# The scale of w_in from sums of magnitudes by ScalarE's accumulator, in place of maxima by VectorE

## The chip, the cores and the metric

The kernel runs on one core of a Trainium2 chip. The time is the device time in microseconds of one execution, the median of three runs. The core has five engines that matter here: TensorE (PE) multiplies matrices, VectorE (DVE) and ScalarE (ACT) work on elements, GpSimd (POOL) does sums and reductions over partitions, and SyncE (SP) issues the transfers by DMA. Each engine works through its own instructions in their order; semaphores make one engine wait for another.

## The reference

Attention with random features comes first, over 8 batches, 8 heads, 576 rows and 64 columns; then a two-layer network over its output, as 4608 rows of 512.

```python
scale = 1.0 / np.sqrt(np.sqrt(D))
q_s, k_s = (q * scale, k * scale)

def phi(x):
    proj = np.einsum('bhsd,md->bhsm', x, omega)      # omega is 128 x 64
    sq = np.sum(x * x, axis=-1, keepdims=True) / 2.0
    h = proj - sq
    h = h - np.max(h, axis=-1, keepdims=True)
    return np.exp(h) / np.sqrt(m)

q_p, k_p = (phi(q_s), phi(k_s))
kv = np.einsum('bhsm,bhsd->bhmd', k_p, v)
z = np.sum(k_p, axis=2)
num = np.einsum('bhsm,bhmd->bhsd', q_p, kv)
den = np.einsum('bhsm,bhm->bhs', q_p, z)[..., None] + 1e-06
x = (num / den).transpose(0, 2, 1, 3).reshape(4608, 512)

h = x @ w_in                                          # 512 x 2048
sp = np.where(h > 20.0, h, np.log1p(np.exp(np.minimum(h, 20.0))))
out = (h * np.tanh(sp)) @ w_out                       # 2048 x 512
```

Everything is float32, in and out.

## The kernel before, in words

**Numbers.** Most matmuls run on float16. Each float32 operand is split into two float16 parts, a high one and what is left, and three products of parts are summed. So that the parts stay in the range of float16, each operand is multiplied by a power of two first. For the activations that factor comes from constants (`HC` is one) and from the scales of the operands; for the weights it comes from the data: from the largest magnitude in `w_in`, and in `w_out`.

**Weights.** Each of the two weight matrices comes as eight blocks of 128 x 1024. A block is loaded as 64-bit words, and `w_task` (from L200) makes float32 out of them: ACT shifts the upper word by a Prelu (L211), DVE the lower one (L213), DVE joins them (L217, its result goes to a tile `w` or `wo`), and DVE reduces the block to the largest magnitude of each partition, one column of `wmax` (L221). When all eight blocks of a matrix are there, `w_scale` (L229) reduces `wmax` once more (`am`) and takes the largest over the partitions: for `w_in` by POOL (`pow2`, L156, which calls L118), for `w_out` by a PE transpose and a matmul that spreads the value again (`pow2_pe`: row_w L136, one_w L139, every_w L148). Then `w_split` (L244) makes the two float16 parts of each block, the high one on ACT (L74), the rest on DVE (L85).

**Rows and chunks.** The 4608 rows go in 18 chunks of 256. For each chunk, `ff_in` (L763, matmuls into `ph`) multiplies by `w_in`, the nonlinearity follows on ACT and DVE (result `g`), and `ff_out` (matmuls into `po`) multiplies by `w_out`. The last three chunks use a scheme with seven products in place of eight (`ff_in7`, `ff_out7`). Chunk 0, and the first feature tiles, are computed in float32 directly, since the split weights don't exist yet: `ff_in` for it reads the unsplit `w` (L782), `ff_out0` (L1113, matmuls at L1129) the unsplit `wo`.

**Features.** `features` (L385) makes a tile of q or k features: PE multiplies by omega (`pq`, `pk`: L426 in float32, L411 in float16), DVE takes the maximum of each row (`mxq`, `mxk`, L436), ACT the exponentials (`eq`, `ek`, L441 and L451). k features are multiplied with v into `pkv` (L500), whose evicted form is `kvf` or `kv`. q features are transposed, by PE in the first tiles (`pt`, L677, evicted as `qp`) and by DMA later (`qp<-qn`), and multiplied with kv (`pn`, L688 and L584); DVE divides (L692 to L698) and gives the rows `x`, whose transpose (`px`, then `xT`) goes into `ff_in`. At the start PE also runs matmuls without a use (`spin`, L101), some of which wait for the same data as real ones.

**Order.** The program is written as generators, each of which yields when it has issued a step; an agenda of slots decides which goes on next, by start tables and by the number that each yields (a later slot). A scheduler with priorities then orders each engine's instructions, and `behind(...)` (L194) ties an instruction behind the n-th matmul of a list of anchors; the tables `AN`, `AO`, `AP` and `AM` hold such numbers for the steps of `w_task`.

Of the kernel before, what the change touches and what calls it, by code (L numbers as in the profile page):

```python
# [9 lines left out]
F16 = mybir.dt.float16  # L10
# [4 lines left out]
AF = mybir.ActivationFunctionType  # L15
ALU = mybir.AluOpType
AX = mybir.AxisListType
# [5 lines left out]
TOP = 2.0 ** 14  # L23
KVC = 2.0 ** -23
TX = 2.0 ** 12
HC = 2.0 ** -22
LNT = math.log(TOP)


# [1 line left out]
def tile_kernel(  # L31
    ctx: ExitStack,
    tc: tile.TileContext,
    qT: bass.AP,
    kT: bass.AP,
    vL: bass.AP,
    omT: bass.AP,
    w_in: bass.AP,
    w_out: bass.AP,
    out: bass.AP,  # L40
):
    nc = tc.nc
    P = 128
# [18 lines left out]
    sb = ctx.enter_context(tc.tile_pool(name="sb", bufs=2))  # L62
# [6 lines left out]
    act, dve, pool = nc.scalar, nc.vector, nc.gpsimd  # L69
# [104 lines left out]
    BW = KT * DF // NB  # L174
# [3 lines left out]
    def flat32(slot):  # L178
        return slot.rearrange("p a b -> p (a b)").bitcast(F32)

    def fetch_w(n, i, dma):
        src = w_src[n](i)


        at = ({0: 0, 1: 1, 2: 2, 3: 3}, {7: 0, 6: 1, 3: 0})[n].get(i)
        if at is not None:
            raw = wo_t[:, 2 * at:2 * at + 2].rearrange("p a b c -> p (a b c)").bitcast(I64)
        else:
            raw = sb.tile([P, BW], I64, tag="g", name=f"raw{i}", bufs=GB)
        dma.dma_start(out=raw.rearrange("p (a b) -> p a b", b=src.shape[2]), in_=src)  # L190
        return raw

    @contextmanager
    def behind(nth, first=0):  # L194
        with ExitStack() as st:
            for ins in anchors.get(nth, ())[first:]:
                st.enter_context(tc.issue_after(ins))
            yield

    def w_task(i, name):  # L200

        n = 0 if name == "wi" else 1
        raw = loaded.pop(f"w{n}_{i}", None) or fetch_w(n, i, w_dma)
        yield W_LOAD
        word = raw.bitcast(I32).rearrange("p (n two) -> p n two", two=2)
        low, high = word[:, :, 0], word[:, :, 1]
        dst = flat32(slots[w_at(n, i)])
        di = dst.bitcast(I32)
        with behind(AP[i] if n == 0 else None):
            m = high.bitcast(F32)  # L210
            act.activation(m, m, AF.Prelu, scale=2.0 ** -112, alpha=-(2.0 ** 32))  # L211
        with behind((AN, AO)[n][i]):
            dve.tensor_single_scalar(out=di, in_=low, scalar=29, op=ALU.logical_shift_right)  # L213
        yield W_GAP
        did("w", n, i)
        with behind((AN, AO)[n][i]):
            dve.scalar_tensor_tensor(  # L217
                out=di, in0=high, scalar=3, in1=di, op0=ALU.logical_shift_left, op1=ALU.bitwise_or
            )
        with behind(AM[i] if n == 0 else None):  # L220
            dve.tensor_reduce(  # L221
                out=wmax[n][:, i:i + 1], in_=dst, axis=AX.X, op=ALU.max, apply_absolute_value=True
            )

    def w_at(n, i):

        return i + 1 if n == 0 else NB + i
# [37 lines left out]
    def did(*key):  # L265
        done[key] = done.get(key, 0) + 1
# [467 lines left out]
    def b_scales(b):  # L734


        if b not in scales:
# [6 lines left out]
            dve.scalar_tensor_tensor(  # L744
                out=us[:, 1:2], in0=s_v, scalar=HC * TX / TOP, in1=s_w[0], op0=ALU.mult, op1=ALU.mult
            )
# [6 lines left out]
    def o_scale(b):  # L753
        us = b_scales(b)
        if b not in done_o:
            done_o.add(b)
            dve.tensor_tensor(out=us[:, 2:3], in0=us[:, 0:1], in1=p_w[1], op=ALU.mult)
            dve.tensor_scalar_mul(us[:, 2:3], us[:, 2:3], 1.0 / (TX * HC))
        return us
# [397 lines left out]
    AO = (None,) * 8  # L1157
    AV = 3
    AN = (None,) * 5 + (31,) * 3
    AM = (None,) * 3 + (31,) * 5  # L1160
    AP = (None,) * 7 + (101,)

    W_LO = ('dddddddd', 'dddddddd')
    W_HI = ('aaaaaaaa', 'aaaaaaaa')
# [26 lines left out]
    wmax = []  # L1191
# [63 lines left out]
    for what in PREL.split():  # L1255
        i = int(what[1:] or 0)
# [12 lines left out]
    for i in range(NB):  # L1269
        start(w_task(i, "wi"), WIS[i])  # L1270
    for i in reversed(range(1, NB)):
        start(w_task(i, "wo"), WOS[i])
# [9 lines left out]
    next(fi, None)  # L1282
    fi, fo = ff_in(1), ff_out0()
    start(w_task(0, "wo"))
    at(slot[0] + W_LOAD + W_GAP + 2, scale_w, 1)
    for j in range(8):
# [75 lines left out]
```

## Time and profile before

| | |
|---|---|
| time, median of 3 runs | 940.65 us (939.26 to 940.75) |
| profiled execution, whole time | 941.74 us |
| its span, first to last instruction | 940.0 us |
| PE busy | 922.9 us, 98 % |
| DVE, ACT, POOL busy | 705.5, 658.9, 214.0 us |
| mean granted TensorE clock | 0.991 of full speed |

The durations below are from the one profiled execution. Its whole time is longer than its span by what lies before the first and behind the last instruction. In a row of a timeline, the time in brackets is how long the engine stood idle before the group, and what it waited for. Instructions on an engine overlap a little, so the distance between the starts of two equal instructions (the pitch) is shorter than the duration of one.

### The profile page before, as it was taken

To read this page: it belongs to the slowest core of one execution; us is meant where nothing else is said; L and a number is where in the kernel's file an instruction comes from. 1 tells how busy PE (TensorE), PEld (TensorE's weight loads), DVE (VectorE), ACT (ScalarE), POOL (GpSimd) and SP (SyncE) were. 2 spreads that over 40 slices of the span, in tenths; PEclk is the share of its full clock that TensorE was granted. 3 is DMA by queue.
4 is the path that set the end of the run, shared out by engine and by line. 5 is a ranking of instruction groups with operands and counts; after the bars stand their busy time and mean duration, and the time that the engine had idled before them with its cause. 6 is when DMAs were issued, how large, how long until landed. Compare 5 with 4: busy or idle time off the path is not lost. (4 is left out here: it accounts for less than half of the span.)

```text
span 940.0 us, 21111 instructions
## 1 busy us (share of the span) xinstructions
PE 922.9 (98%) x8795; PEld 690.8 (73%) x8795; DVE 705.5 (75%) x1234; ACT 658.9 (70%) x873; POOL 214.0 (23%) x134
## 2 busy tenths in 40 slices
PE   9699989999999999999999999999999999999998
PEld 6588865777777777777777777777777776679997
DVE  4799898686678688887688856878688666658774
ACT  5668976678786878778677786778787766345442
POOL 0000023252242123321233133231242232200000
PEclk9799999999999999999999999999999999999999
DMA  9867323532452255423543255422533146973521
GB/s 297 273 217 223 101 66 86 105 77 68 105 109 75 77 97 145 89 74 93 104 111 95 80 104 122 109 77 75 121 81 91 34 107 148 226 201 91 158 69 45
DMA packets 153055, 108.69 MB, mean 116 GB/s; under 512 B 112832, under 2 KB 125248, under 8 KB 152960
## 3 DMA queue, kind: packets, MB, share of 16 engines
q1 hardware_dynamic: 152640, 106.75, 44.3%
q8 instruction: 69, 1.13, 0.5%
q10 hardware_dynamic: 320, 0.59, 0.2%
q14 instruction: 26, 0.21, 0.1%
HBM read 63.14 MB, written 17.83 MB: 86 GB/s over the span
## 5 line engine op out<-in xcount | busy, mean ns | idle before, releaser
L782 PE MATMUL ph<-xT,w 128*128 128x256 f16 (+1 forms) x2816 | 342.2, 278 | 0.0
L1111 PE MATMUL po<-wo,g 128*128 128x512 f16 x1344 | 308.5, 379 | 0.0
L782 PEld LDWEIGHTS <-w 128*128 128x128 f16 x2688 | 260.7, 98 | 46.1 <-issue 0.6
L1111 PEld LDWEIGHTS <-g 128*128 128x128 f16 x1344 | 127.3, 98 | 132.7
L83 POOL TENSOR_TENSOR sq<-fq,sq 64x1024 f16<-64x1024 f32 x31 | 70.7, 2280 | 252.8 <-ACT sq L74 175.3
L969 ACT ACTIVATE h<-ph,us 128x512 f32<-128x512 f32 (+3 forms) x152 | 83.4, 573 | 50.6 <-PE ph L782 49.7
L85 DVE SCALAR_TENSOR_TENSOR g<-h,us,g 128x1024 f16<-128x1024 f32 (+3 forms) x76 | 98.7, 1309 | 15.2 <-ACT g L74 14.9
L83 POOL TENSOR_TENSOR sk<-fk,sk 64x1152 f16<-64x1152 f32 x24 | 59.4, 2474 | 91.8 <-ACT sk L74 84.2
L83 POOL TENSOR_TENSOR xs<-x,xs 128x512 f16<-128x512 f32 (+1 forms) x35 | 40.8, 1165 | 153.0 <-DVE xs L76 102.2
L969 ACT ACT_TABLE_LOAD x56 | 71.8, 1283 | 1.0
L451 ACT ACT_TABLE_LOAD x53 | 68.0, 1283 | 4.2 <-DVE ek L445 3.3
L436 DVE TENSOR_REDUCE mxq<-pq 128x4 f32<-128x512 f32 x72 | 46.7, 682 | 24.3 <-PE pq L411 23.3
L83 DVE TENSOR_TENSOR qn<-eq,qn 128x1024 f16<-128x1024 f32 x31 | 39.2, 1264 | 29.7 <-ACT qn L74 29.6
L919 PEld LDWEIGHTS <-w 128*128 128x128 f16 x1008 | 59.0, 98 | 3.0 <-issue 0.4
L74 ACT ACTIVATE g<-h,us 128x1024 f16<-128x1024 f32 (+3 forms) x64 | 58.1, 932 | 0.9
L451 ACT ACTIVATE ek<-ek,lnt 128x1152 f32<-128x1152 f32 x24 | 30.1, 1256 | 40.2 <-DVE ek L445 40.1
L436 DVE TENSOR_REDUCE mxk<-pk 128x4 f32<-128x512 f32 (+1 forms) x96 | 49.6, 548 | 9.8 <-PE pk L426 4.0
L83 DVE TENSOR_TENSOR kp<-ek,kp 128x1152 f16<-128x1152 f32 x24 | 32.8, 1366 | 25.7 <-ACT kp L74 25.7
L1058 PEld LDWEIGHTS <-gb 128*128 128x128 f16 x504 | 48.3, 98 | 5.2
L83 POOL TENSOR_TENSOR vb<-vf,vb 128x640 f16<-128x640 f32 x24 | 37.3, 1556 | 56.5 <-DVE vb L76 42.4
L451 ACT ACTIVATE eq<-eq,lnt 128x1024 f32<-128x1024 f32 x31 | 35.6, 1149 | 18.9 <-DVE eq L445 18.7
L969 ACT ACTIVATE h<-h,us 128x1024 f32<-128x1024 f32 (+2 forms) x16 | 14.7, 932 | 48.3 <-DVE h L929 48.3
(185 smaller groups left out, 1373.9 us busy)
## 6 DMA issues: line engine op xcount, KB each, us to landing
w<-ds SPq DMA_DIRECT2D x48, 256.0 KB, 3.5
vf<-in_vL_dram SPq DMA_DIRECT2D x32, 325.0 KB, 3.4
out_dram<-o SPq DMA_DIRECT2D x36, 256.0 KB, 2.4
fq<-in_qT_dram SPq DMA_DIRECT2D x31, 256.0 KB, 3.5
fk<-in_kT_dram SPq DMA_DIRECT2D x24, 256.0 KB, 3.7
raw<-in_w_out_dram SPq DMA_DIRECT2D x5, 1024.0 KB, 8.1
wo<-in_w_in_dram SPq DMA_DIRECT2D x4, 1024.0 KB, 10.9
raw<-in_w_in_dram SPq DMA_DIRECT2D x4, 1024.0 KB, 15.0
```

Source lines behind the costliest of these rows:

```text
L74: act.activation(out, in_, AF.Copy, scale=scale)
L83: eng.tensor_tensor(out=out, in0=in_, in1=hi, op=ALU.subtract)
L85: eng.scalar_tensor_tensor(out=out, in0=in_, scalar=scale, in1=hi, op0=ALU.mult, op1=ALU.subtract)
L436: sub = dve.tensor_reduce(out=mx[:, lo:hi], in_=pp[:, :m, :], axis=AX.X, op=ALU.max, negate=by_act)
L451: last = act.activation(e, e, AF.Exp, bias=lnt)
L782: last = nc.tensor.matmul(out=ph[:, i, :], lhsT=wi(a, k, f) if c else wi0(k, f), rhs=xT[c][:, y, k, :] if c else xT0()[:, k, :], start=n = ...
L919: last = nc.tensor.matmul(out=ph[:, i, :], lhsT=left(gr, op_l, i, a, k), rhs=x_region(c, r)[:, y, k0 + k, :], start=n == 0, stop=n == len( ...
L969: act.activation(h[:, :, lo:hi], ph[:, :, lo:hi], AF.Mish, scale=us[:, 0:1])
L1058: nc.tensor.matmul(out=ps, lhsT=gT[c, n][:, i, a, f, :], rhs=rhs, start=f == 0 and (a, y) == (1, 0), stop=f == FG - 1 and (a, y) == (0, 0),)
L1111: last = nc.tensor.matmul(out=po[i], lhsT=gT[c, gr][:, a, f % FG, i * P:(i + 1) * P], rhs=wo(y, f), start=f == 0 and (a, y) == parts[0], s ...
```

## The change

For `w_in` (n == 0) the column of `wmax` is no longer DVE's largest magnitude of a block's partition but the sum of the 1024 magnitudes: ACT takes Abs of the block into a scratch tile `rough`, which nothing reads, and its accumulator gives the sum. The largest over blocks and partitions is taken as before and rounded to a power of two. `w_out` keeps its maxima. As the sums are larger than the maxima, the parts of `w_in` become smaller, and the constant `HC` in the factors of the activations goes from 2^-22 to 2^-20. The scratch tile has the tag of `xs`, of which there are two buffers.

```diff
-HC = 2.0 ** -22
+HC = 2.0 ** -20
...
-        with behind(AM[i] if n == 0 else None):
-            dve.tensor_reduce(
-                out=wmax[n][:, i:i + 1], in_=dst, axis=AX.X, op=ALU.max, apply_absolute_value=True
-            )
+        if n == 0:
+            yield WSUM[i]
+            rough = sb.tile([P, BW], F16, tag="xs", name=f"rough{i}", bufs=2)
+            with behind(AP[i]):
+                act.activation(rough, dst, AF.Abs, accum_out=wmax[n][:, i:i + 1])
+            return
+        dve.tensor_reduce(
+            out=wmax[n][:, i:i + 1], in_=dst, axis=AX.X, op=ALU.max, apply_absolute_value=True
+        )
...
-    AM = (None,) * 3 + (31,) * 5
     AP = (None,) * 7 + (101,)
+    WSUM = (0,) * 8
```

The instructions of all engines stand in another order in about the first 175 us, and in the same order behind that. Lines behind the change have numbers that are five higher than before.

On DVE, ahead of the maxima of q's first tile (mxq) and before that tile's exponentials, the rows were these (w_104 is a block of `w_in`, vam and p_v belong to the scale of v):

```order
L217 SCALAR_TENSOR_TENSOR w_104<-wo,w_104 128x1024
L327 TENSOR_REDUCE vam_358<-vmx_353 128x1
L213 TENSOR_SCALAR w_105<-wo 128x1024
L161 TENSOR_SCALAR p_v_362<-allm_v_360 128x1
L221 TENSOR_REDUCE wmax_121<-w_104 128x1
L125 TENSOR_SCALAR p_v_362<-p_v_362 128x1
L436 TENSOR_REDUCE mxq_330<-pq_0_331 128x4
```

And now:

```order
L217 SCALAR_TENSOR_TENSOR w_104<-wo,w_104 128x1024
L332 TENSOR_REDUCE vam_359<-vmx_354 128x1
L213 TENSOR_SCALAR w_105<-wo 128x1024
L161 TENSOR_SCALAR p_v_363<-allm_v_361 128x1
L441 TENSOR_REDUCE mxq_331<-pq_0_332 128x4
L125 TENSOR_SCALAR p_v_363<-p_v_363 128x1
```

The maximum of block w_104 is gone from the place ahead of mxq, and so is that of the block before it, further up.

On ACT, between the transposed rows of chunk 0 (xT) and the exponentials of q's tile 2 (eq) with what follows them, the rows were these:

```order
L716 ACTIVATE xT_297<-px_481 128x4x128
L716 ACTIVATE xT_297<-px_487 128x4x128
L211 ACTIVATE raw_159<-raw_159 128x1024
L74 ACTIVATE g_0_634<-ph_0_0_0_635 128x512
L441 ACTIVATE eq_520<-pq_0_522,mxq_521 128x128 x4
L441 ACTIVATE eq_520<-pq_4_523,mxq_521 128x128 x4
L74 ACTIVATE qp_564<-pt_0_565 128x512
L74 ACTIVATE g_0_634<-ph_0_0_2_657 128x512
L441 ACTIVATE eq_532<-pq_0_534,mxq_533 128x128 x4
```

And now:

```order
L721 ACTIVATE xT_297<-px_491 128x4x128
L211 ACTIVATE raw_155<-raw_155 128x1024
L211 ACTIVATE raw_157<-raw_157 128x1024
L211 ACTIVATE raw_159<-raw_159 128x1024
L224 ACTIVATE rough_516,wmax_121<-w_108 128x1024
L224 ACTIVATE rough_521,wmax_121<-w_109 128x1024
L224 ACTIVATE rough_526,wmax_121<-w_110 128x1024
L446 ACTIVATE eq_528<-pq_0_530,mxq_529 128x128 x4
L446 ACTIVATE eq_528<-pq_4_531,mxq_529 128x128 x4
L446 ACTIVATE eq_540<-pq_0_542,mxq_541 128x128 x4
L446 ACTIVATE eq_540<-pq_4_543,mxq_541 128x128 x4
L74 ACTIVATE qp_572<-pt_0_573 128x512
```

Two Prelu (raw_155 and raw_157) that stood ahead of xT, and three Abs, now stand between xT and the exponentials, and all sixteen exponentials stand ahead of the first evicted qp; the g casts come later.

On PE, at the same place, from the last product with omega (pq) to the transposes (pt):

```order
L426 MATMUL pq_4_535<-om_f,fq_507 128x128
L782 MATMUL ph_0_0_0_635<-xT_297,w_103 128x256 x7
L782 MATMUL ph_0_0_2_657<-xT_297,w_104 128x256 x6
L677 MATMUL pt_0_565<-ident,eq_520 128x128 x4
L782 MATMUL ph_0_0_2_657<-xT_297,w_104 128x256 x2
L782 MATMUL ph_0_1_0_682<-xT_297,w_105 128x256
L677 MATMUL pt_1_571<-ident,eq_520 128x128 x4
```

And now:

```order
L431 MATMUL pq_4_543<-om_f,fq_512 128x128
L787 MATMUL ph_0_0_0_643<-xT_297,w_103 128x256 x4
L682 MATMUL pt_0_573<-ident,eq_528 128x128 x4
L787 MATMUL ph_0_0_2_665<-xT_297,w_104 128x256
L682 MATMUL pt_1_579<-ident,eq_528 128x128 x4
L787 MATMUL ph_0_0_2_665<-xT_297,w_104 128x256 x2
L682 MATMUL pt_0_586<-ident,eq_540 128x128 x4
```

Fewer matmuls of chunk 0 stand ahead of the first transposes (a matmul in float32 is two instructions in the profile); the others follow behind pn.

On PE, around every_w, the rows were these:

```order
L136 MATMUL row_w_1116<-ident,am_w_1114 1x128
L677 MATMUL pt_1_1108<-ident,eq_1042 128x128
L1129 MATMUL po_0_1387<-wo,g_1_785 128x512
L677 MATMUL pt_1_1108<-ident,eq_1042 128x128 x2
L1129 MATMUL po_0_1387<-wo,g_1_785 128x512
L148 MATMUL every_w_1122<-one_w_1118,idle 128x1
L688 MATMUL pn_0_1133<-kvf_162,qp_1101 64x65
```

And now:

```order
L787 MATMUL ph_0_1_2_1171<-xT_508,w_105 128x256
L787 LDWEIGHTS w_105
L787 MATMUL ph_0_1_2_1171<-xT_508,w_105 128x256
L148 MATMUL every_w_1130<-one_w_1126,idle 128x1
L693 MATMUL pn_0_1141<-kvf_162,qp_1109 64x65
```

No po of chunk 0 stands around every_w any more; matmuls of the next chunk's `ff_in` do.

## Rows read from the trace of the kernel before

**Rows 1.** The page: busy time of PE with its share of the span and its instructions, beside those of the other engines; then PE and the granted clock in 40 equal slices of the span, in tenths.

```profile
PE 922.9 (98%) x8795; PEld 690.8 (73%) x8795; DVE 705.5 (75%) x1234; ACT 658.9 (70%) x873; POOL 214.0 (23%) x134
...
PE   9699989999999999999999999999999999999998
...
PEclk9799999999999999999999999999999999999999
```

**Rows 2.** The waits of PE over the whole span: who waited for whom; us in total, times, longest us.

```profile
PE spin L101 <- ACT eq L441: 7.3, 1, 7.3
PE pn L584 <- DMA qp<-qn: 2.5, 3, 1.9
...
PE every_w L148 <- DVE one_w L139: 0.8, 1, 0.8
```

**Rows 3.** Windows: stretch, its length, busy time (and instructions) of PE, PEld, DVE, ACT and POOL, then the granted clock, the share of the DMA engines and GB/s.

```profile
25.00:26.00 1.00, 0.00 (x0) 0.00 (x0) 1.00 (x3) 0.34 (x1) 0.00 (x0) 1.00 1.05 385
26.00:27.00 1.00, 0.00 (x0) 0.00 (x0) 1.00 (x2) 0.61 (x1) 0.00 (x0) 0.81 1.03 381
27.00:28.00 1.00, 0.00 (x0) 0.00 (x0) 0.87 (x3) 0.55 (x1) 0.50 (x1) 0.50 1.05 387
...
39.00:40.00 1.00, 1.00 (x7) 0.69 (x5) 0.00 (x0) 0.93 (x3) 0.00 (x0) 0.50 1.05 269
40.00:41.00 1.00, 1.00 (x8) 0.81 (x7) 0.00 (x0) 1.00 (x4) 0.00 (x0) 0.86 1.02 296
```

**Rows 4.** The timeline of PE from 0 to 62 us: start, duration of the group, what it is, and the idle time before it.

```profile
14.36 2.44 PE L500 MATMUL pkv<-vf,ek 128*128 128x65 f32 x20
...
21.54 2.06 PE L426 MATMUL pq<-om_f,fq 64*128 64x128 f32 x32
30.87 1.22 PE L101 MATMUL spin<-eq,ident 128*128 128x256 f32 x2 [7.27 <-ACT eq L441]
31.88 4.36 PE L500 MATMUL pkv<-vf,ek 128*128 128x65 f32 x20
...
49.48 5.88 PE L782 MATMUL ph<-xT,w 128*128 128x256 f32 x26
55.83 0.66 PE L677 MATMUL pt<-ident,eq 128*128 128x128 f32 x4 [0.48 <-ACT eq L441]
```

**Rows 5.** The timeline of DVE, from 20 to 30 us.

```profile
20.76 1.21 DVE L221 TENSOR_REDUCE wmax<-w 128x1 f32<-128x1024 f32 x1
...
25.99 1.21 DVE L217 SCALAR_TENSOR_TENSOR w<-wo,w 128x1024 int32<-128x1024 int32 x1
...
28.22 1.21 DVE L221 TENSOR_REDUCE wmax<-w 128x1 f32<-128x1024 f32 x1
29.35 0.14 DVE L125 TENSOR_SCALAR p_v<-p_v 128x1 f32<-128x1 f32 x1
29.41 0.68 DVE L436 TENSOR_REDUCE mxq<-pq 128x4 f32<-128x512 f32 x1
```

**Rows 6.** The timeline of ACT, from 26 to 72 us.

```profile
26.39 1.16 ACT L211 ACTIVATE wo<-wo 128x1024 f32<-128x1024 f32 x1 [1.05 <-DMA wo<-in_w_in_dram]
30.19 2.18 ACT L441 ACTIVATE eq<-pq,mxq 128x128 f32<-128x128 f32 x8 [2.64 <-DVE s_v L127]
...
41.36 0.27 ACT L74 ACTIVATE kvf<-pkv 128x130 f32<-128x130 f32 x1
41.52 2.15 ACT L211 ACTIVATE raw<-raw 128x1024 f32<-128x1024 f32 x2
...
46.13 0.60 ACT L716 ACTIVATE xT<-px 128x512 f32<-128x512 f32 x1 [0.70 <-PE px L715]
...
54.64 1.14 ACT L441 ACTIVATE eq<-pq,mxq 128x128 f32<-128x128 f32 x4 [1.23 <-DVE mxq L436]
...
61.77 1.28 ACT L74 ACTIVATE w<-w,s_w 128x1024 f16<-128x1024 f32 x1
...
64.86 0.74 ACT L74 ACTIVATE xs<-x 128x512 f16<-128x512 f32 x1
...
71.24 0.60 ACT L74 ACTIVATE g<-ph 128x512 f32<-128x512 f32 x1 [0.87 <-PE ph L782]
```

**Rows 7.** Groups of instructions by line and form, from 0 to 110 us: count, then busy us and mean ns of one, then idle time before them.

```profile
L221 DVE TENSOR_REDUCE wmax<-w 128x1 f32<-128x1024 f32 x8 | 9.5, 1208 | 0.0
L211 ACT ACTIVATE raw<-raw 128x1024 f32<-128x1024 f32 x9 | 10.4, 1165 | 0.1
```

**Rows 8.** The timeline of PE from 117 to 161 us, and behind the dots the window from 144 to 146 us (columns as in rows 3).

```profile
119.98 0.38 PE L148 MATMUL every_w<-one_w,idle 1*128 1x1 f32 x2 [0.81 <-DVE one_w L139]
...
133.97 5.32 PE L1129 MATMUL po<-wo,g 128*128 128x512 f32 x12
141.17 0.92 PE L584 MATMUL pn<-kv,qp 128*128 128x65 f16 x24 [1.89 <-DMA qp<-qn]
...
143.95 14.19 PE L1129 MATMUL po<-wo,g 128*128 128x512 f32 x30
...
159.29 0.92 PE L584 MATMUL pn<-kv,qp 128*128 128x65 f16 x24 [0.29 <-DMA qp<-qn]
...
144.00:146.00 2.00, 2.00 (x4) 0.97 (x4) 1.95 (x6) 1.17 (x2) 1.27 (x1) 0.50 0.00 0
```

**Rows 9.** Transfers issued from 55 to 85 us: how many, and the median us from issue to landing.

```profile
xT<-xs SPq DMA_TRANSPOSE x2, 4.2
```

## The prediction, made blind

> **What bounds the kernel now.** I read the busy shares first. TensorE (PE) is busy 98 % of the span and every other engine 76 % or less [rows 1]; with 922.9 us busy in a span of 940.0, all that an edit elsewhere can give back at once is the 17 us in which PE stands still, and what PE does at a lower clock. The reader is to see in the forty slices that PE falls below nine tenths in the second slice (23.5 to 47 us), the sixth (117.5 to 141) and the last one, and the granted clock (PEclk) in the second alone. The list of PE's waits names the gaps [rows 2]: 7.3 us for the first exponentials of q, 2.5 us for three transposes of qn by DMA, 0.8 us for the scale of w_out (every_w); a fourth, 0.48 us for the second lot of exponentials, stands in the timeline [rows 4]. All lie in the first 160 us, and so do the instructions that the change moves: by the order of the instructions both kernels are alike on every engine from about 175 us on.
>
> Then the place of the long wait. PE ends pq at 21.54 + 2.06 = 23.60 and starts again at 30.87 [rows 4]. PEclk in the windows is 1.00 until 26, 0.81 in the microsecond from 26, 0.50 from 27 on (1.2 GHz instead of 2.4), and it is 0.50 until 40, then 0.86 [rows 3]. So the clock fell some 3.2 us into the wait, and came back near 40.7, some 9.8 us after PE was at work again. What that costs is in PE's own rows: the same twenty pkv take 2.44 us before and 4.36 behind the wait [rows 4].
>
> **The change part by part.** Removed are eight maxima of VectorE (DVE), 1208 ns each with a pitch of 1.13 [rows 5, 7]; added are eight Abs on ScalarE (ACT), each over 128x1024 f32, with a sum. The trace of before has no ACT row that sums. Nearest is the Prelu over the same form: 1165 ns by itself [rows 7], two in 2.15, so a pitch of 1.02 to 1.04 [rows 6]. Lower end 1.04. Upper end: the sum is written by a step of its own, as long as the smallest ACT row, 0.27, so 1.16 + 0.27 = 1.4 [rows 6]. I take 1.15, near the lower end, since the work on the elements is the same. The other edit, a power of two in a constant, changes no instruction: 0.
>
> The Trainium skill ("ScalarE: Activation LUTs", Rules for kernel authors) says of simple functions such as max and add that they belong on VectorE, up to about three times as fast in bf16. This case's row disagrees for f32 and a reduction: 1208 ns for DVE's maximum, 1165 for ACT's Prelu [rows 7]. By the rule ACT would lose some 2 us with each of the eight; by the row it is an even exchange, and what counts is which engine is waited for.
>
> *Term 1, the wait at 23.6: −2.3 us.* In DVE's queue two maxima of w_in stand ahead of q0's first mxq, at 20.76 and at 28.22, mxq itself at 29.41 [rows 5]. Without both it starts at 29.41 − 2 × 1.13 = 27.15, ends with its 0.68 near 27.8, and the exponentials, which started 0.78 behind mxq's start (30.19, [rows 6]), at about 27.9. PE, 0.68 behind these, restarts near 28.6. In place of the maxima two Abs stand ahead of eq on ACT. The second needs w's second word operation, at 25.99 with its maximum still ahead of it [rows 5], so 24.9 to 26.1 now; it ends near 27.3, before mxq is out: hidden, by 0.5 us. ACT's Prelu at 26.39 waits for its DMA [rows 6] and comes behind. Bounds −1.9 (the Abs at 1.4, and Prelu in the way) and −2.6. The wait becomes 5.0.
>
> *Term 2, the clock: 0.* 5.0 is still more than 3.2, so the clock falls as before and I let it come back as long after the restart. Were it to come back at the same 40.7, PE would have 2.3 us more of half clock, +1.2; if earlier, −1.0. Both ends kept.
>
> *Term 3, from 44 to 60 us: +1.55.* Here ACT's order changes most. Before, behind the two xT (the second at 46.13), one Prelu follows, then a g cast that waits for ph, then the exponentials of q's tile 2 at 54.64 [rows 6]; these waited for DVE. After, three Prelu and three Abs stand between xT and these exponentials. xT ends at 46.73 − 2.3 = 44.4, and 44.4 + 3 × 1.04 + 3 × 1.15 = 51.0, first four done at 52.15 (DVE, three maxima freer, is no longer late). PE has eight f32 ph ahead of the first pt instead of fourteen: before, it ran dry at 55.35 [rows 4], so now at 55.35 − 2.3 − 6 × 0.452 = 50.3 (thirteen ph took 5.88, 0.452 each). It waits 52.15 − 50.3 = 1.8 instead of 0.48: +1.35; and with only one or two ph between the pts I add 0.2 for shorter waits. The w_in cast of 61.77 [rows 6] comes earlier, the g casts later; ph has nine matmuls still to do, all of which stand behind pn: no loss, moved. Bounds: Abs at 1.04, +1.2; at 1.4, +2.3.
>
> *Term 4, from 60 to 98 us: +0.3.* PE ran without a wait. DVE is now some 5 us ahead, ACT as much later by three Abs; I allow one small wait for an evicted kv. In SP's queue one load of w_out now stands behind the two transposes of xs; these land 4.2 after their issue [rows 9], and ACT has 0.87 to spare at that place [rows 6]. Ends 0 and 4.2 − 0.9 = +3.3.
>
> *Term 5, from 98 to 163 us: −3.0.* In PE's order seven f32 po matmuls (14 instructions; twelve in 5.32, 0.443 each: 6.2 us) move from around every_w to behind it, and so the scale of w_out is early: every_w's 0.81 goes. The first pn of L584 waits 1.89 for its transposed qp [rows 8]; the chain before it starts earlier against PE, half of it goes, −0.9. From that pn to the next (141.17 to 159.29) a chain of about 17 us (mxq, exponentials, qn, transpose) decides; PE fills it with thirty po in 14.19 us, part of that at half clock (PEclk 0.50 from 144 to 146), and waits 0.29 only [rows 8]. After, the stretch lasts as long, but po moved in front of it no longer lengthens the time before; what PE loses to the clock falls into time that the chain sets anyway, −1.3. Together −0.8 − 0.9 − 1.3. Bounds: −0.5, if both transposes stay as late against PE as now, and −4.2 if the whole 1.89 goes and the lost clock too.
>
> Sum: −2.3 + 0 + 1.55 + 0.3 − 3.0 = −3.45. The profiled execution was 941.74 around a span of 940.0, so 938.3 for such an execution; it stands 1.1 above the median of the runs, 940.65, and on that scale the forecast is 937.2.
>
> **The rivals.** *Cancelled:* DVE and ACT get their hands free or full early, but the late waits hang on q's chain and on transposes, which the change doesn't shorten. For it: the waits of L584 are put down to DMA, not to DVE [rows 2]. Against it: every_w's wait is DVE's. Then term 5 is −0.5, the sum −0.95: 939.7.
>
> *Slower:* the new wait before pt is long enough for a second fall of the clock. Place: PE's wait behind the eight ph near 50. It is 1.8 by my sum; from 3.2 on the clock falls, as it did at 26.8 [rows 3]. That is reached if eq comes 1.4 later, so if an Abs costs about 1.6 instead of 1.15, or DVE or a load is late by as much. Price: 1.4 for the wait, and about ten microseconds of work at half clock, as from 30.87 to 40.7, +5: −3.45 + 6.4 = +2.95, so 943.6. Against it: 1.6 lies above my upper end.
>
> *Larger gain:* the shorter first wait lets the clock come back sooner, or not fall, and both transposes are early. −2.3 − 1.0 + 1.2 + 0 − 4.2 = −6.3, 934.3; without a fall of the clock, some 5 less still. The row says that it falls after 3.2 and the wait would be 5.0, so this needs a second mistake of mine in term 1.
>
> *Not what it says:* Abs could need another table and load it eight times, or its scratch tile, which shares buffers with xs, could hold xs up. In the order no load of a table is added, four fewer stand there, and xs is first written at 64.9 in the trace, behind all eight: neither is given a chance of its own.
>
> **How the numbers follow.** Forecast 0.52 (937.2), cancelled 0.25 (939.7), slower 0.15 (943.6), larger gain 0.08 (934). The forecast alone with its bounds, terms partly against each other, is 934.5 to 940.2. The range for eight in ten takes the cancelled case whole and the near part of the slower one: 933.5 to 943.0. A change under 0.2 %, 1.9 us, can't be told from none here. Faster, below 938.75: most of the forecast (0.42), the larger gain, and a little of the cancelled: 0.55. Same, up to 942.55: the rest of these and a little of the slower: 0.25. Slower: 0.20.
>
> **What would show it.** Right: PE's wait for the first eq near 5.0 instead of 7.3; Abs rows of about 1.15; q's second eq near 51; a PE wait of about 1.8 before pt with PEclk 1.00; no wait at every_w; and a shift against before that stays constant from 175 us to the end. Wrong: a second slice of PEclk at 0.5 near 52, an Abs row at 1.4 or more, or the waits of L584 unchanged.

## The result, and the profile after

The changed kernel takes 946.79 us (945.72 to 948.43, six runs) against 940.17 us of the kernel before, now by six runs: a ratio of 1.007, interval 1.006 to 1.008. It is 6.6 us slower, where 3.5 us faster was forecast, and outside the range. The profiled execution was 947.19 us around a span of 945.4, against 941.74 and 940.0.

The page of the changed kernel, as in [rows 1]:

```profile
PE 924.6 (98%) x8795; PEld 691.9 (73%) x8795; DVE 702.2 (74%) x1226; ACT 662.5 (70%) x885; POOL 215.9 (23%) x134
...
PE   9899978999999999999999999999999999999998
...
PEclk9799998999999999999999999999999999999999
```

PE is busy 1.7 us longer for the same 8795 matmuls, and stands still 20.8 us instead of 17.1: 1.7 + 3.7 = 5.4, the whole difference of the spans. The second slice, 6 before, is now 8; the sixth and seventh are 7 and 8, where they were 8 and 9, and PEclk is 8 in the seventh. So something was won near 30 us, and more was lost between 120 and 165. The waits of PE, as in [rows 2], say what:

```profile
PE pn L589 <- DMA qp<-qn: 8.4, 3, 5.2
PE spin L101 <- DVE s_v L127: 3.3, 1, 3.3
...
PE every_w L148 <- DVE one_w L139: 1.3, 1, 1.3
PE pq L431 <- ACT ek L446: 0.9, 1, 0.9
PE pt L682 <- ACT eq L446: 0.8, 1, 0.8
```

The first long wait is 3.3 us and not 7.3 (with 0.9 of a new one just before it, 4.1); the waits for q's transposes grew from 2.5 to 8.4. −3.1 + 5.9, and 0.8 for every_w and pt, make the 3.7 of standing still but for 0.1. PE's timeline (start, us, what, the wait before), as in [rows 4, 8]:

```profile
28.14 1.22 PE L101 MATMUL spin<-eq,ident 128*128 128x256 f32 x2 [3.25 <-DVE s_v L127]
...
51.18 0.65 PE L682 MATMUL pt<-ident,eq 128*128 128x128 f32 x4 [0.77 <-ACT eq L446]
...
111.31 0.38 PE L148 MATMUL every_w<-one_w,idle 1*128 1x1 f32 x2 [1.35 <-DVE one_w L139]
...
116.32 1.06 PE L416 MATMUL pq<-om,sq 128*128 128x128 f16 x16
117.22 8.02 PE L787 MATMUL ph<-xT,w 128*128 128x256 f16 x72
125.08 5.32 PE L1134 MATMUL po<-wo,g 128*128 128x512 f32 x12
135.59 1.44 PE L589 MATMUL pn<-kv,qp 128*128 128x65 f16 x24 [5.20 <-DMA qp<-qn]
...
139.29 14.86 PE L1134 MATMUL po<-wo,g 128*128 128x512 f32 x34
157.07 1.50 PE L589 MATMUL pn<-kv,qp 128*128 128x65 f16 x24 [2.92 <-DMA qp<-qn]
158.38 6.83 PE L1134 MATMUL po<-wo,g 128*128 128x512 f32 x10
165.06 3.60 PE L1134 MATMUL po<-w,g 128*128 128x512 f32 x8
168.49 1.06 PE L416 MATMUL pq<-om,sq 128*128 128x128 f16 x16
```

Two moments compare the kernels with the same work done. In the kernel before they are these, with the po that stood ahead of the first:

```profile
99.79 1.88 PE L1129 MATMUL po<-wo,g 128*128 128x512 f32 x4
...
105.33 1.94 PE L1129 MATMUL po<-wo,g 128*128 128x512 f32 x4
...
117.07 1.02 PE L1129 MATMUL po<-wo,g 128*128 128x512 f32 x2
...
118.14 1.02 PE L1129 MATMUL po<-wo,g 128*128 128x512 f32 x2
...
120.91 1.13 PE L1129 MATMUL po<-wo,g 128*128 128x512 f32 x2
...
125.21 1.06 PE L411 MATMUL pq<-om,sq 128*128 128x128 f16 x16
...
162.70 1.06 PE L411 MATMUL pq<-om,sq 128*128 128x128 f16 x16
```

At the pq of 116.32 PE has done all that it had done before at 125.21, but for seven po in float32 (fourteen instructions of 0.443 us, 6.2): it is 8.9 − 6.2 = 2.7 us ahead. At the pq of 168.49 the po are all done in both kernels; before, that was at 162.70. PE is 5.8 us behind. So 8.5 us are lost in between, and behind that nothing changes (the spans differ by 5.4). One more thing is seen there: at the end ten instructions of po take 6.83 us, where twelve take 5.32 at full clock, and the windows show why (columns as in [rows 3]):

```profile
136.00:138.00 2.00, 2.00 (x30) 1.94 (x28) 1.22 (x6) 0.00 (x0) 0.00 (x0) 0.50 0.00 0
...
158.00:160.00 2.00, 2.00 (x13) 1.20 (x11) 1.30 (x6) 0.69 (x2) 0.00 (x0) 0.50 0.00 0
160.00:162.00 2.00, 2.00 (x4) 0.73 (x3) 1.45 (x1) 0.37 (x1) 1.15 (x1) 0.50 0.00 0
```

Behind each of the two waits PE works at half clock for a while.

What makes qp late stands in DVE's timeline. PE's pq (of q's tile 5, the first with a transpose by DMA) ends at 117.2, and its maxima mxq come 6.2 us later:

```profile
118.05 2.22 DVE L85 SCALAR_TENSOR_TENSOR g<-h,us,g 128x1024 f16<-128x1024 f32 x1
120.19 3.14 DVE L85 SCALAR_TENSOR_TENSOR wo<-wo,s_w 128x1024 f16<-128x1024 f32 x1
123.37 1.29 DVE L441 TENSOR_REDUCE mxq<-pq 128x4 f32<-128x512 f32 x2
```

In the kernel before, pq ended at 126.1 and mxq began 1.7 later:

```profile
125.67 1.25 DVE L85 SCALAR_TENSOR_TENSOR wo<-wo,s_w 128x1024 f16<-128x1024 f32 x1
...
127.85 1.29 DVE L436 TENSOR_REDUCE mxq<-pq 128x4 f32<-128x512 f32 x2
```

DVE has come forward by 4.5 us (127.85 to 123.37), PE by 8.9, since it no longer does the seven po first. From mxq to pn the chain is even shorter than before (12.2 us against 13.3). POOL, at the same time:

```profile
118.03 1.16 POOL L83 TENSOR_TENSOR xs<-x,xs 128x512 f16<-128x512 f32 x1 [3.27 <-ACT xs L74]
119.54 2.71 POOL L83 TENSOR_TENSOR sq<-fq,sq 64x1024 f16<-64x1024 f32 x1 [0.35 <-POOL xs L83]
```

DVE's two split instructions, 1.28 us elsewhere, are stretched where a POOL instruction runs beside them.

### The profile page after: what moved, and what is told of

Same layout as the page of the kernel before. It is cut to its first block, busy times and chain, and to the rows that moved or that the text cites. A ratio compares the mean times of both kernels' runs of the same rounds, so it can differ in the third digit from the quotient of the medians.

```text
span 945.4 us, 21118 instructions
## 1 busy us (share of the span) xinstructions
PE 924.6 (98%) x8795; PEld 691.9 (73%) x8795; DVE 702.2 (74%) x1226; ACT 662.5 (70%) x885; POOL 215.9 (23%) x134
## 3 DMA queue, kind: packets, MB, share of 16 engines
q8 instruction: 69, 1.13, 0.5%
## 5 line engine op out<-in xcount | busy, mean ns | idle before, releaser
L85 DVE SCALAR_TENSOR_TENSOR g<-h,us,g 128x1024 f16<-128x1024 f32 (+3 forms) x76 | 101.6, 1348 | 15.3 <-ACT g L74 14.9
```

The lines of the kernel that those rows point to most:

```text
L85: eng.scalar_tensor_tensor(out=out, in0=in_, scalar=scale, in1=hi, op0=ALU.mult, op1=ALU.subtract)
```

## The experiments

Two theories stood against each other. *Order:* the loss is made where PE's po no longer stand ahead of the late pn, whatever computes the maxima. *Work:* eight Abs make ScalarE late by some 8 us and so everything that hangs on it. A third thing, DVE's queue with the stretched instruction, could add to the first or be all of it. Times are medians, beside runs of the kernel before on the same chip.

**Earlier po in the changed kernel.** `ff_out0` is begun in the loop ahead of its own:

```diff
     for j in range(8):
         next(fi, None)
         step()
+        if j >= 5:
+            next(fo, None)
         step()
```

> The changed kernel with ff_out0 begun three blocks earlier, so that 12 po of chunk 0 stand ahead of the first pn of the later q tiles (6 in the changed kernel), 20 between that and the second (17) and none behind it (9); all eight Abs stay. Theory O (order): the loss is PE's order at 130 to 165 us, where po that had filled PE now stands behind pn; the two waits of 5.2 and 2.9 us shrink to under 0.5 each, the clock does not fall a second and third time (some 4 us), so about 935 us, below both kernels. Rival W (work): eight Abs of 1.04 us each make ScalarE late, and all that hangs on it; order doesn't matter: 945 to 947, the waits only move.

943.51 us, ratio 1.0046 (1.0032 to 1.006). The two waits go, as order says: the first pn isn't waited for at all, the second 0.40, and PE starts the later `ff_out` at 162.60, 4.5 us ahead of the kernel before. But the fourth such pn, that of q's tile 8, then waits 5.2, and the clock falls behind it (expectations of later runs call it the third; the third isn't waited for):

```profile
175.61 0.91 PE L589 MATMUL pn<-kv,qp 128*128 128x65 f16 x24
...
184.52 1.50 PE L589 MATMUL pn<-kv,qp 128*128 128x65 f16 x24 [5.17 <-DMA qp<-qn]
```

So the place of the loss is as order has it, and the time is not: 5.2 of the 8.1 us came back two tiles later.

**The po late in the kernel before.** No Abs, the maxima on DVE; only the matmuls of `ff_out0` are tied:

```diff
+                    with ExitStack() as st:
+                        st.enter_context(tc.issue_after(pq_last["q5"].ins))
                         last = nc.tensor.matmul(
```

> The kernel before, VectorE's maxima and all, with ff_out0's matmuls tied behind the last pq of q's tile 5: PE's order around the two pn becomes that of the changed kernel (6 po, pn, 17 po, pn, 9 po). Theory O: the kernel before gets the loss without the change: 946 to 949 us, with two long waits for qp<-qn and a half clock behind each. Rival W: no Abs, so about 940.

946.27 us, ratio 1.0069 (1.0056 to 1.0081): as slow as the changed kernel, without the change. PE's rows:

```profile
120.84 1.06 PE L412 MATMUL pq<-om,sq 128*128 128x128 f16 x16
...
136.23 0.92 PE L585 MATMUL pn<-kv,qp 128*128 128x65 f16 x24 [1.31 <-DMA qp<-qn]
...
156.60 1.48 PE L585 MATMUL pn<-kv,qp 128*128 128x65 f16 x24 [3.19 <-DMA qp<-qn]
...
166.78 1.06 PE L412 MATMUL pq<-om,sq 128*128 128x128 f16 x16
```

A loss of this size thus needs no Abs, which speaks against work. But it isn't the changed kernel's loss in the same place. Only one of the two waits became long (4.7 us of waits for qp, against 8.4). By the two moments used above: at 120.84 PE is 4.4 us earlier than the kernel before, but owes the seven po, 6.2 us, so that it is 1.8 behind already. Near 101 and 105 us, where po had stood, it now waits 1.1 and 0.5 us for ek. From there to 166.78 it loses 2.3 more, where the changed kernel lost 8.5.

**DVE's queue in the changed kernel.** The rest of w_out's first split block goes behind the maxima of q's tile 5:

```diff
-            rest(dve, dst[:, 1], src, dst[:, 0], s)
+            with ExitStack() as st:
+                if (n, i) == (1, 7):
+                    st.enter_context(tc.issue_after(mx_last["q5"].ins))
+                rest(dve, dst[:, 1], src, dst[:, 0], s)
```

> The changed kernel with the rest of w_out's first split block tied behind the maxima of q's tile 5 on VectorE (one instruction of 3.1 us that stood ahead of them); PE's order stays. Theory S (VectorE's queue): mxq starts some 3 us earlier and the first wait falls from 5.2 to about 2.1; the second stays at 2.9: about 943.5. Theory O alone, with the chain set elsewhere: 946.5.

943.52 us, ratio 1.0041 (1.0028 to 1.0053), as expected of the queue. mxq begins at 120.61, 2.8 us earlier. The first wait is 1.30 instead of 5.20 (with a new one of 1.7 ahead of it, for h), the second 2.98. The moved instruction now took 1.28 us, at 123.01, when POOL's had ended.

**Earlier po in the kernel before.** The edit of the first experiment, without the change.

> The kernel before with ff_out0 begun three blocks earlier, as in the first of these runs; maxima by VectorE. Prices the earlier po without the change. Theory O: its waits for qp<-qn were only 1.9 and 0.3, and the half clock from 143 to 147 us; so at most 3 us better: 937 to 940, and the first of these runs lies 2 to 4 us below it, by the earlier start at 28 us. Rival W: the first of these runs lies above it by some 6 us.

948.37 us, ratio 1.0097 (1.0083 to 1.0112): a miss by some 10 us. The two waits stay (1.89 and 0.39) and the fourth pn, of q's tile 8, waits 5.2, as in the first experiment. Against that one it says something else: with po begun three blocks earlier in both, the kernel with the sums is 4.9 us faster than the one with the maxima. That is the opposite of what work expects.

**Both mends together,** `ff_out0` two blocks earlier (`j >= 6`) and DVE's rest behind mxq, in the changed kernel:

> The changed kernel with both mends: ff_out0 begun two blocks earlier and the rest of w_out's first split block behind the maxima of q's tile 5. Each alone gave 943.5. If the two losses are separate places they add: 940 to 941. If PE is held by the chains of q's tiles 5 to 7 as a whole, so that what is mended at the first pn comes back as a wait at a later one (5.2 us at the third pn in the first run of this study), it stays at 943 or more.

937.46 us, ratio 0.9967 (0.9954 to 0.998): faster than both kernels, by 2.7 us against the one before and 9.3 against the changed one. It is below the 940 to 941 expected of two separate losses too; that sum took 943.5 for the earlier po, which is the time with three blocks, and two blocks alone, run later, take 940.97. PE's rows:

```profile
133.46 0.92 PE L594 MATMUL pn<-kv,qp 128*128 128x65 f16 x24 [1.31 <-DMA qp<-qn]
...
153.60 0.92 PE L594 MATMUL pn<-kv,qp 128*128 128x65 f16 x24 [0.38 <-DMA qp<-qn]
154.36 3.68 PE L1139 MATMUL po<-w,g 128*128 128x512 f32 x8
157.87 1.06 PE L420 MATMUL pq<-om,sq 128*128 128x128 f16 x16
```

All po are done at 157.87; before it was 162.70, so PE is 4.8 us ahead. The waits for qp are 2.5 us, as in the kernel before, and behind these two the clock stays at 1.00. Of the 4.8, 2.8 were there at the pq of 116.22, the early gain; most of the rest is half clock that the profiled execution of the kernel before had from 142.7 to 146.1 (0.67 from 142 to 144 us, 0.50 to 146 [rows 8], 0.98 to 148; it costs 1.7 us) and this one has not. The medians differ by less, 2.7. Of the sixteen executions of the kernel before beside the run that completes the square below, five have a mean clock of 0.991, as the profiled one, and take 0.8 us more on average than the eleven with 0.992 to 0.994; that half clock may be absent in these, but no trace of one was kept.

**The sums for two blocks only,** the two Abs that stand where DVE's maxima held q0 up:

```diff
-        if n == 0:
+        if n == 0 and i in (0, 1):
             yield WSUM[i]
```

> The sums by ScalarE for w_in's first two blocks alone (the two Abs that stand in VectorE's way ahead of q0's maxima); the other six keep VectorE's maxima, so that the scale comes from two sums and six maxima. PE's order near the late pn is that of the kernel before but for one or two po. Theory of the chains: the early wait falls from 7.3 to about 4 and the late order is the old one; 938 to 940, but not the whole 3 us, since the chain of q's tile 5 doesn't come earlier by as much. Rival (any Abs on ScalarE costs): above 941.

941.11 us, ratio 1.0012 (1.0002 to 1.0023), above the 938 to 940 expected. The early wait fell to 3.5 and 0.9; the first late pn waits 4.1 instead of 1.9, and the clock is at 0.50 from 140 to 146. Again the gain at the start comes back there. The rival bound of 941 is met by a hair and settles nothing.

**No wait for the chains,** in both kernels:

```diff
-    out=pn[lo:hi, i, :], lhsT=qp[:, a, h, lo:hi], rhs=kv[b][:, h, y, :],
+    out=pn[lo:hi, i, :], lhsT=qp[:, a, h, lo:hi] if t > 7 else ident.bitcast(F16)[:, 0:hi - lo], rhs=kv[b][:, h, y, :],
```

> The changed kernel in which pn of q's tiles 5, 6 and 7 multiplies by the unit matrix's words in place of the transposed qn: PE doesn't wait for the three chains (those rows of the output are not attention's; the transposes are still made). Theory of the chains: the waits of 8.1 us and the half clock behind them go, and the change shows its worth: about 934 us, 2.5 to 5 below the same edit of the kernel before. Rival (the change costs elsewhere too): not below that.

> The kernel before with the same edit: pn of q's tiles 5 to 7 doesn't wait for the transposed qn. Theory of the chains: 2.2 us of waits and some 1.5 us of half clock go: 936 to 938.

939.18 and 938.26 us (ratios 0.9983 and 0.9979). The second came out as expected, the first did not: it gained 7.6 us, so that the chains are the larger part of the loss, but it ran into waits of 2.5 and 1.6 us for DVE (pq behind x, every_v), and it is 0.9 us slower than the second, not 2.5 to 5 faster. So the theory of the chains is too narrow: without these waits PE still catches up with DVE, and the early gain isn't seen in the time. Which of DVE's work is late there was not separated.

**The square.** Earlier po by two blocks alone, which with the three runs above completes a square:

> The changed kernel with ff_out0 begun two blocks earlier (8 po ahead of the first late pn, 20 between, 4 behind) and nothing else; with the run of both mends, the run of the VectorE mend alone and the changed kernel it makes a square. If po's place and VectorE's queue are two separate losses: 946.8 - 6 = about 940.8. If the wait stays at the first pn (mxq still behind the 3.1 us instruction, po short by two) or comes back at the third: 942 to 944.

940.97 us, ratio 1.0008 (0.9998 to 1.0018). Changed 946.8, DVE mend 943.5, po mend 941.0, both 937.5: −3.3 and −5.8 apart, −9.3 together. In the medians the two mends add. They don't mend two separate waits, though: in the profiled execution of this run (943.13 us; the twelve go from 939.2 to 944.7) the first wait is still 3.49 with half clock behind it, and the second 0.39, so the po take something off both.

**Both mends in the kernel before.**

> The kernel before with both mends, VectorE's maxima kept: what the mends give without the change. If the change is worth its early gain (the first wait 7.3 to 4.1, which is 3.1 us) once the late order is mended: 940 to 941, against 937.5 with the sums. Rival: the mends alone make the gain, 937 to 938 here too, and the sums are worth nothing.

945.54 us, ratio 1.0054 (1.0041 to 1.0066). Neither expectation holds: the mends, worth 9.3 us to the changed kernel, cost the one before 5.2. Its waits for qp are 1.2, 3.2 and, at 796 us, 1.3, where they were 1.9, 0.3 and 0.3. In its second chain ACT waits 1.86 us for DVE ahead of the split of w_out that stands in front of qn (at 152.87), and DVE's split at 150.28 takes 2.50 beside a POOL instruction; in the kernel before ACT doesn't wait there. With the same mends the sums are 8.1 us faster than the maxima; but since the mends fit one order and not the other, that is no price of the sums.

**Three blocks instead of two,** with the DVE mend:

> The changed kernel with both mends, ff_out0 begun three blocks earlier instead of two. In the first run of this study three blocks gave a wait of 5.2 us at the third late pn, whose chain met a long instruction beside GpSimd's. If the three blocks make that wait: about 941 to 943; if the first split block did: 937.

943.74 us, ratio 1.004 (1.0027 to 1.0052). The third block makes the wait of 5.1, at the fourth pn. Between the maxima and the last part of qn of q's tile 8, ACT loads four tables in that order (1.28 each), three with two blocks, and DVE's last part of qn takes 3.17 us beside a POOL instruction, 1.22 with two blocks.

**Place in the program alone.** DVE's maximum in place of each Abs, at the Abs' place and without the anchor:

```diff
-                act.activation(rough, dst, AF.Abs, accum_out=wmax[n][:, i:i + 1])
+                dve.tensor_reduce(
+                    out=wmax[n][:, i:i + 1], in_=dst, axis=AX.X, op=ALU.max, apply_absolute_value=True
+                )
```

> The changed kernel with VectorE's maximum in place of each Abs: only the step's place in the program and the missing anchor are changed against before. Theory (VectorE's work ahead of q0's maxima is what the early wait is made of): the early wait is 7 us again, 940 to 945 by where the late order falls; rival (the place in the program alone gives the early gain): 4 us there.

945.82 us, ratio 1.0058 (1.0046 to 1.007). The early wait is 7.3 again, as in the kernel before, and the late waits for qp are 5.6. The early gain is thus DVE's freed time, not the place; and the late loss needs no Abs.

**What stretches DVE's instruction.** First a tie that didn't hold:

```diff
-        rest(by("lo", nth), ks[D:P], f, ks[0:D])
+        with ExitStack() as st:
+            if name == "q7":
+                st.enter_context(tc.issue_after(mx_last["q5"].ins))
+            rest(by("lo", nth), ks[D:P], f, ks[0:D])
```

> The changed kernel with one GpSimd instruction (sq of q's tile 7) tied behind VectorE's maxima of tile 5; VectorE's order up to there and PE's order stay. In the changed kernel that sq ran from 119.5 to 122.3 us, and VectorE's split of w_out beside it took 3.1 us, 1.28 where nothing ran on GpSimd. If GpSimd's instruction is what stretches it: about 1.3 us, maxima 1.9 us earlier, the first late wait 5.2 becomes about 3.3, 943 to 945 us. If the length comes from VectorE's own queue: 3.1 us again and 946 to 947.

946.39 us, ratio 1.007 (1.0051 to 1.0088). POOL's instruction ran at its old place, at 120.49, beside DVE's (which took 3.15): this tie made POOL wait for nothing on DVE. The run is the changed kernel once more. Then through its data, by the ScalarE cast that it reads:

```diff
-        cast(by("hi", nth), ks[0:D], f)
+        with ExitStack() as st:
+            if name == "q7" and "q5" in ex_last:
+                st.enter_context(tc.issue_after(ex_last["q5"].ins))
+            cast(by("hi", nth), ks[0:D], f)
```

> In the run before this one the tie did not hold the GpSimd instruction back (it ran at the same place), so it told nothing. Here the ScalarE cast that GpSimd's instruction reads (sq of q's tile 7) stands behind the exponentials of tile 5 instead; VectorE's order up to the maxima of tile 5 and PE's stay those of the changed kernel. If GpSimd's instruction stretches VectorE's split of w_out: that takes about 1.3 us instead of 3.1, the maxima come 1.9 earlier, the first late wait 5.2 becomes about 3.3, 943 to 945 us. If the length is VectorE's own: 3.1 us again and 946 to 947.

944.64 us, ratio 1.0051 (1.0039 to 1.0063), and the rows of DVE:

```profile
120.36 1.27 DVE L85 SCALAR_TENSOR_TENSOR wo<-wo,s_w 128x1024 f16<-128x1024 f32 x1
121.67 1.29 DVE L445 TENSOR_REDUCE mxq<-pq 128x4 f32<-128x512 f32 x2
...
130.24 3.02 DVE L85 SCALAR_TENSOR_TENSOR g<-h,us,g 128x1024 f16<-128x1024 f32 x1
```

and of POOL:

```profile
129.93 2.25 POOL L83 TENSOR_TENSOR sq<-fq,sq 64x1024 f16<-64x1024 f32 x1 [10.57 <-ACT sq L74]
```

The split of w_out takes 1.27 us, the first late wait is 3.30, and another DVE instruction of the same kind, beside the moved POOL instruction, now takes 3.02. It is POOL's instruction that stretches DVE's.

## Why the prediction was wrong, point by point

*What bounds the kernel:* right. PE is 98 % busy in both kernels, and the whole difference is PE's standing still and its half clock.

*Term 1 (−2.3):* right in mechanism and nearly in size. PE restarts at 28.14 instead of 30.87, −2.7, and the wait is 4.1 in two parts (forecast 5.0); DVE's two maxima were in the way, and the run with DVE's maxima at the new place has the wait of 7.3 back. Abs is cheaper than taken: a row of 1.05 to 1.09 and one of 0.19 to 0.24 that overlaps it, a pitch of 1.04 (46.85, 47.89 and 48.93 us), the lower end:

```profile
48.93 1.09 ACT L224 ACTIVATE rough<-w 128x1024 f16<-128x1024 f32 x1
49.87 0.24 ACT L224 ACTIVATION_READ_ACCUMULATOR rough<-w 128x1 f32 x1
49.97 4.24 ACT L446 ACTIVATE eq<-pq,mxq 128x128 f32<-128x128 f32 x16
```

*Term 2 (0):* the clock fell as forecast, to 0.50 near 26.5, and came back near 36.7 (the window from 36 to 37 us has 0.64), 8.6 us behind the restart. Before it was 9.4 and not 9.8: a mean of 0.86 in the microsecond from 40 is 0.28 us at half clock and the rest at full, so the clock came back at 40.3 and not at 40.7; by the same reckoning 0.81 in the microsecond from 26 puts its fall at 26.6, 3.0 us into the wait and not 3.2. That is 0.8 us less at half speed, −0.4, inside the bounds.

*Term 3 (+1.55):* the right place and wait, a smaller size: q's second exponentials start at 49.97 (forecast 51.0), and PE waits 0.77 before pt (1.8).

*Term 4 (+0.3):* nothing was lost there. At 116 us PE was 2.7 us ahead in all, with every_w's wait grown to 1.35, where the terms up to there came to 0.45, or 1.25 with every_w's wait gone.

*Term 5 (−3.0):* this step failed, in sign. From 116 to 168 us the kernel lost 8.5. None of its three parts came: every_w's wait, which was to go (−0.8), grew from 0.81 to 1.35; the first pn's wait, which was to halve (−0.9), grew from 1.89 to 5.20; and the half clock, which was to cost nothing (−1.3), came twice. Two sentences of it were wrong. "The chain before it starts earlier against PE": it starts later against PE. I counted the seven po as work that moves from a place ahead of every_w to a place behind it, and did not ask what they had been doing there, which was to keep PE back until DVE had q's tile 5 ready. PE came to pq 8.9 us earlier, DVE to its maxima only 4.5 earlier; what the po had filled became a wait of 5.2. And "after, the stretch lasts as long": the stretch between the two pn grew from 18.1 to 21.5 us, so po behind it gained nothing, and most of the last ten instructions ran at half clock. That the loss needs no Abs was seen twice, in the kernel before with the po alone moved (946.3) and in the changed kernel with DVE's maxima (945.8); that it hangs on po and DVE's queue, by the two mends (937.5). How much of the 8.5 is due to each alone is shown by the medians only.

The rule of the Trainium skill that I weighed in the prediction ("ScalarE: Activation LUTs", Rules for kernel authors: simple functions belong on VectorE) would have said slower, and the result is slower, but not by it: ACT's Abs with its sum has a pitch of 1.04 us and DVE's maximum 1.13. A rule that does bear on the loss, and that I left out, stands in "SBUF — State Buffer", Who interferes with whom: a VectorE instruction with two inputs in SBUF contends with a GpSimd instruction that reads SBUF, and `tensor_reduce` never does. The trace agrees: DVE's split (two inputs in SBUF) takes 1.27 us alone and 3.14 beside POOL's, while the maxima (TENSOR_REDUCE, 1.29 for two) kept that time in the run with the DVE mend, where they ran at 120.61 beside POOL's sq of 119.85 (they read PSUM, so this is no full test).

*The rivals.* None was the right one. "Slower" had the nearest price (943.6, measured 946.8), by luck, for its place was wrong: a second fall of the clock near 50 us, by Abs at 1.6. The clock did fall again, near 135.7 and 156.2 (0.93 from 134 to 136 us, 0.55 from 156 to 158). The 3.2 us from which, by this rival, the clock falls were read from one wait and are no rule: in [rows 8] it stands at 0.50 behind a wait of 1.89, and in the changed kernel it fell 1.6 us behind the end of pq (24.9), then 5.3 and 2.1 us behind the start of the two late waits. "Cancelled" had the right doubt, that the late waits hang on q's chain, which the change doesn't shorten; it lacked that PE's distance to that chain can shrink or grow by the work that stands ahead.

What stays open: why the two kernels' planned order puts the seven po where it does, beyond that they are filler with a later place in the program; why the mends make the kernel before slower by 5.2 us, of which the waits and the clock show the place and only part of the reason; what the sums are worth by themselves. In pairs with the same edits they are 4.9 and 8.1 us faster and 0.9 slower than the maxima: each edit meets another order, so no pair is their price.

## What to carry to other kernels

Where an order is planned from estimates, price a change by the filler that it moves: for each wait that is small now, ask what work stands ahead of it, and what the wait would be without. An engine freed at the start only helps as far as the slowest producer of the next wait comes forward as well; here PE came to q's tile 5 earlier by 8.9 us and DVE by 4.5. After such a change, look at the first wait behind the gained stretch and put the filler and the producer's queue right again: here two small edits turned 6.6 us of loss into 2.7 of gain. And try them anew on each order: the same two edits cost the kernel before 5.2 us.

## What the runs showed of the hardware

A DVE instruction of 1.27 us (split of 128x1024, two inputs in SBUF) takes 2.8 to 3.2 when a POOL tensor_tensor of 64x1024 began just ahead of it (2.84 in the kernel before, at 130.38; 3.14, 3.15 and 3.02 above); even one of 128x1 took 2.08 us, at 112.70, when POOL's ran from 112.64 to 114.76. A wait of PE is not paid by its length alone: behind the 5.20 and the 2.92 us of the changed kernel PE worked at 0.50 for some 3 and 6 us, but behind one of 2.17 us (the first late pn of the run with DVE's maxima at the new place) the clock stayed at 1.00, and behind the 1.89 us in the kernel before it fell, some 1.5 us after PE was at work again (0.67 from 142 to 144 us, then [rows 8]).
